# A two-pass channel scaling kernel: 26 rows fewer kept between the passes and loaded again ahead of the second pass, and the arena moved to the front of its pool

## The chip, the cores and the metric

The kernel runs on one core of one Trainium2 chip. A core has a matrix engine (PE, or TensorE), a vector engine (DVE), a scalar engine (ACT), a general engine (POOL), a queue processor (SP) that here does nothing but issue DMA transfers, 16 DMA engines, an on-chip memory of 128 partitions (SBUF) and a small accumulator memory (PSUM). The metric is the device time of one execution, in microseconds (us); lower is better. The time before is 722.07 us, the median of three runs (721.76, 722.07 and 722.96).

## What is computed

The input `x` is one image of 384 by 384 points with 384 channels in bf16, 113.2 MB. The mean of every channel over all points is multiplied by one number `w1d`, put through a sigmoid, and every point is then scaled, channel by channel, by the result:

```python
g = jnp.einsum("bhwc->bc", x) / (H * W)
s = jax.nn.sigmoid(g * w1d[0])          # k = 1: the padding and the loop over i fall away
return x * s[:, None, None, :]
```

No output can be written before all of the input has been read and summed. The input doesn't fit into SBUF, so a part of it has to be read twice.

## The kernel before, in words

**Rows and chunks.** The 147,456 points are cut into 1152 "rows". A row is one point, 384 channels or 768 bytes, on each of the 128 partitions: 98,304 bytes in all. A chunk of n rows is one DMA; `view` gives each partition n points that lie behind each other in HBM, so that a DMA is 128 runs of n times 768 bytes, eight on each of the 16 DMA engines. The trace calls such a run a packet.

**The arena.** One tile, `arena`, of 275 rows per partition (line 181) holds nearly everything. `QS` (line 152) and `RAW` (line 160) lay it out: five areas for packed groups, then the pieces U (8 rows), V (8), A (39), Y (8) and T (8). The pool gives its tiles addresses in the order in which they are made, each rounded up to 32 bytes per partition. What the framework itself keeps ends at byte 16,512 of a partition. Before, `ones` (256 bytes), `w_bf`, `w_sc`, `worst` and `odd` (32 each) stand ahead of the arena, which so begins at byte 16,896, which is 66 times 256. A row is three times 256 bytes, so every row begins at a multiple of 256 bytes.

**Pass one** reads all 1152 rows. PE sums them into one PSUM bank: `sum_rows` issues a matmul with a matrix of ones for each row. Three things happen to a row after that:

- 785 rows (`N_STREAM`) are only streamed: they are overwritten, and read again in pass two.
- 296 rows are kept packed, four rows in the room of three, in groups: `fold` (line 272) hides the bits of a fourth row in the exponent bits of three others, with DVE and ACT.
- 71 rows (`N_RAW`, line 164) are kept as they are, "raw", in U, V, A, Y and T.

The streamed rows of the end of pass one go through three slots of 13 rows in A (`SLOTS`, line 368; `S1`, `S2`, `S3`), in the order that the list `BETWEEN` gives (line 380). After the last of them, `take_raw` (line 414) loads the 71 raw rows into the same three slots, then V, U, Y and T. Y, T, U and V are scratch or landing room of the folds until then.

**The turn.** When the last matmul is done, ACT computes the sigmoid (line 422) into `s_bf`. From then on DVE can scale rows in place (`scale`, line 429, one instruction for n rows) and SP can store them (`store`, line 439).

**Pass two** is laid out by a planner that runs when the kernel is built (lines 540 to 717). It steps a simulated clock by 0.05 us, with a cost for each row moved (`ROW`, 0.2267 us), each load (`PER_LOAD`, 0.112) and each store (`PER_STORE`, 0.061), and a model of DVE's times (`TS`, `TT`). It keeps `landed`, the pieces that are in SBUF and can be scaled, in order; `moves`, the transfers that are under way; `turns`, the steps that unpack a folded group; and `idle`, the arena rows that are free. When a run of free rows is long enough (line 700), it issues a load of the next streamed rows into it. The order in which the planner emits is the order of each engine's queue; the waits are put in by the class `Flow` from the rows that each step reads and writes. All loads and stores of rows are issued by SP, on one queue and strictly in that order: an issue that waits for its rows holds all behind it. Each DMA uses one of 24 semaphores in turn.

At the start of pass two `landed` holds the raw rows, in the order Y, T, U, V and A (lines 594 to 599), in eight pieces of 4, 4, 8, 8, 8, 13, 13 and 13 rows.

Of the kernel before, what the change touches and what calls it, by code (L numbers as in the profile page):

```python
# [127 lines left out]
def kernel(  # L128
# [12 lines left out]
    P = nc.NUM_PARTITIONS  # L141
    B, H, W, C = x.shape
# [5 lines left out]
    bf16, f32, u16, u32 = x.dtype, mybir.dt.float32, mybir.dt.uint16, mybir.dt.uint32  # L148
# [8 lines left out]
        areas.append((base, 3 * q))  # L157
        base += 3 * q
    RAW = {}
    for name, n in (("U", 8), ("V", 8), ("A", 39), ("Y", 8), ("T", 8)):  # L160
        RAW[name] = (base, n)
        base += n
    ROWS = base
    N_RAW = sum(n for _, n in RAW.values())
    U, V, A, Y, T = (RAW[n][0] for n in "UVAYT")

    BANKED = len(QS)
    PS = 3 * Q_BANKS
# [2 lines left out]
    pool = ctx.enter_context(tc.tile_pool(name="sb", bufs=1))  # L171
    psum = ctx.enter_context(tc.tile_pool(name="psum", bufs=1, space=bass.MemoryType.PSUM))

    pieces = [(g, lo, min(PIECE, q - lo)) for g, q in enumerate(QS) for lo in range(0, q, PIECE)]

    ones = pool.tile([P, P], bf16, name="ones")
    w_bf = pool.tile([1, 1], bf16, name="w_bf")
    w_sc = pool.tile([P, 1], f32, name="w_sc")
    worst = pool.tile([P, 1], f32, name="worst")
    odd = pool.tile([P, 1], bf16, name="odd")  # L180
    arena = pool.tile([P, ROWS, C], bf16, name="arena")
    s_bf = pool.tile([P, C], bf16, name="s_bf")
    zeros = pool.tile([P, P], bf16, name="zeros")
    seen = pool.tile([P, 2 * len(pieces)], f32, name="seen")
    odd_i = pool.tile([P, 1], mybir.dt.int32, name="odd_i")
    bank0 = psum.tile([P, nc.PSUM_BANK_SIZE_BYTES // 4], f32, name="bank0")
    acc, votes = bank0[:, 0:C], bank0[:, C : C + 1]
# [6 lines left out]
    def view(t, r0, n):  # L194
        return t[r0 * P : (r0 + n) * P, :].rearrange("(p r) c -> p r c", r=n)

    def rows(lo, n):
        return [("a", r) for r in range(lo, lo + n)]
# [3 lines left out]

    N_STREAM = RPP - N_RAW - sum(4 * q for q in QS)
    r = N_STREAM
    c_group = []
    for q in QS:
        c_group.append((r, 4 * q))
        r += 4 * q
    c_raw = (r, N_RAW)
    assert r + N_RAW == RPP  # L210

# [3 lines left out]
    def load(chunk, a, lo=0, hi=None):  # L215

        r0, n = chunk
        hi = n if hi is None else hi
        fl.add(
            "SP",  # L220
            lambda: nc.sync.dma_start(out=arena[:, a : a + hi - lo, :], in_=view(xf, r0, n)[:, lo:hi, :]),  # L221
            writes=rows(a, hi - lo), dma=True,
        )

    def sum_rows(a, n):
        def emit(i, first, last):
            return nc.tensor.matmul(acc, lhsT=ones[:], rhs=arena[:, i, :], start=first, stop=last)  # L227

        for i in range(a, a + n):
            first, last = summed[0] == 0, summed[0] == RPP - 1  # L230
            fl.add(
                "PE", lambda i=i, f=first, l=last: emit(i, f, l),
                reads=[("a", i), "ones"], writes=["bank0"],
            )
            summed[0] += 1
# [132 lines left out]
    SLOTS = [(A + i, 13) for i in range(0, 39, 13)]  # L368
# [3 lines left out]
    S1, S2, S3 = ([slot] for slot in SLOTS)  # L372
    B3, B4, AA = ([area] for area in (areas[3], areas[4], (A, 39)))

    def halves(area):
        a, n = area
        return [(a, n // 2), (a + n // 2, n - n // 2)]
# [4 lines left out]
        ([], B3), ([], B4),  # L382
        ([], B3), ([], AA),
        ([], halves(areas[4])), ([], S1 + S2 + S3),
        (S1, S2, S3 + S1), (S2, S3, S1 + S2 + S3),
    ]
    between = sum(n for b in BETWEEN[1:] for where in b for _, n in where)
    at = 0
    for g, q in enumerate(QS[:BANKED]):
        for lo in range(0, q, 2 * PIECE):  # L390
            n = min(2 * PIECE, q - lo)
# [19 lines left out]
            at += 1  # L411
    assert streamed[0] == N_STREAM

    def take_raw(a, n):
        load(c_raw, a, a - U, a - U + n)
        sum_rows(a, n)

    for a, n in SLOTS + [(V, 8), (U, 8), (Y, 8), (T, 5), (T + 5, 3)]:
        take_raw(a, n)
    assert summed[0] == RPP  # L420

    fl.add(
# [6 lines left out]
    def scale(a, n):  # L429
        v = arena[:, a : a + n, :]  # L430
        fl.add(
            "DVE",
            lambda: nc.vector.tensor_tensor(  # L433
                out=v, in0=v, in1=s_bf[:, None, :].to_broadcast([P, n, C]), op=Op.mult
            ),
            reads=rows(a, n) + ["s_bf"], writes=rows(a, n),
        )
# [46 lines left out]
    def TT(n):  # L484
        return 0.15 + 0.2 * n
# [54 lines left out]
    ROW, PER_LOAD, PER_STORE = 0.2267, 0.112, 0.061  # L540
    LAT, SEEN, DT = 2.0, 1.5, 0.05
    PENDING, MERGE = 24.0, 12.0
    BIG, CAP, PART, LOW, LAST = 32, 48, 16, 9.0, 4.0
    BANKS_AT = 2
    now = dve_at = 0.0
    moves, waiting, over, acts = deque(), deque(), deque(), deque()
    landed = deque()
    idle = [False] * ROWS
    todo = 0
# [18 lines left out]
    def send(chunk, a, lo, hi, then, known=None):  # L568

        waiting.append((dve_at, hi - lo, then, chunk, a, lo, [] if known is None else known))  # L570

    def backlog():
        return sum(e[1] for e in moves) + ROW * sum(e[1] for e in waiting)

    def split(n, m):
        k = -(-n // m)
        cuts = [n * i // k for i in range(k + 1)]
        return list(zip(cuts, cuts[1:]))
# [12 lines left out]
        return f  # L591


    landed.append((c_raw, Y, Y - U, 4, False))
    landed.append((c_raw, Y + 4, Y - U + 4, 4, True))
    landed.append((c_raw, T, T - U, 8, True))
    landed.append((c_raw, U, 0, 8, True))
    for e, n in ((0, 8), (8, 13), (21, 13), (34, 13)):
        landed.append((c_raw, V + e, 8 + e, n, True))

    HALVES = (T, U)
    half = [True, True]
# [46 lines left out]
    while True:  # L649

        if dve_at <= now:
            ahead = backlog()
            can = bool(turns)
            if not can and (ahead >= PENDING or not landed):
                can = start_pair()
                if can and not asked:
                    verdict()
                    asked = True
            if landed and (ahead < PENDING or not can):
                chunk, a, lo, n, end = landed.popleft()  # L660
                scale(a, n)
                dve_at = now + TT(n)
                since = (a, lo) if since is None else since
                if end or ahead < MERGE:
                    b, first = since
                    send(chunk, b, first, lo + n, stored(b, lo + n - first))
                    since = None
            elif can:
                f, t, then = turns.popleft()
                f()  # L670
                dve_at = now + t
                if then:
                    then()
        while waiting and waiting[0][0] <= now:
            _, n, then, chunk, a, lo, known = waiting.popleft()
            known.append(store(chunk, a, lo, lo + n))
            moves.append([now + LAT, n * ROW + PER_STORE, then])
        if out_rows == total and not checked and all(half):
            checked = True
            fl.add("POOL", again, reads=["odd_i", "s_bf"], writes=rows(Y, N_OVER), after=written)  # L680
        while over and over[0][0] <= now:
            over.popleft()[1]()

        got = runs()
        if bank_at is None and len(line) <= len(QS) * 2 - BANKS_AT and got and max(got)[0] >= PS:
            a = max(got)[1]
            for i in range(a, a + PS):
                idle[i] = False
            back = arena[:, a : a + PS, :].rearrange("p r c -> p (r c)")
            for i, bk in enumerate(banks):  # L690
                lo, hi = i * BANK, min((i + 1) * BANK, PS * C)
                copy_bank(i, bk[:, 0 : hi - lo], back[:, lo:hi], [("bank", i)], rows(a, PS))
            bank_at = (a, now + 5.0)
            got = runs()

        if got and todo < N_STREAM:
            n, a = max(got)
            n = min(n, CAP, N_STREAM - todo)
            ahead = backlog()
            if n >= BIG or n == N_STREAM - todo or (ahead < LOW and n >= 8) or ahead < LAST:  # L700
                chunk = (todo, n)
                todo += n
                load(chunk, a)
                for i in range(a, a + n):
                    idle[i] = False
                parts = [(chunk, a + e, e, f - e, f == n) for e, f in split(n, PART)]
                moves.append([now + LAT, n * ROW + PER_LOAD, lambda parts=parts: landed.extend(parts)])

        if moves and moves[0][0] <= now:
            moves[0][1] -= DT  # L710
            if moves[0][1] <= 0:
                over.append((now + SEEN, moves.popleft()[2]))
        else:
            stall += DT
        if not (moves or waiting or over or landed or line or turns) and todo == N_STREAM:
            break
        now += DT
# [34 lines left out]
```

## Time and profile before

| | |
|---|---|
| median of three runs | 722.07 us |
| the profiled execution: its own time, span | 722.96 us, 721.2 us |
| DMA bytes, mean rate over the span | 303.87 MB, 421 GB/s |
| read from HBM, written to it | 190.41 MB, 113.25 MB |
| loads of rows, stores of rows | 82, 56 |
| DVE busy, PE busy, ACT busy | 69%, 30%, 16% |
| last 16 matmuls of the sum start, first scaling starts | 267.8 us, 271.2 us |
| last DMA packets | about 718 us |

The page counts one profiled execution. Its part 2 cuts the span into 40 slices of 18 us; the row DMA gives the mean busy share of the 16 DMA engines in tenths. A finer table, by windows of one microsecond, gives the same share as a number for each (a little over 1 is possible, as a packet is counted where it starts), and GB/s. In the timeline, a line gives start, duration, engine, source line, operation and how many instructions were merged, and in brackets the idle time before and what ended it.

### The profile page before, as it was taken

Reading aid. Unit: us, or ns where it says so; the run is one execution under the profiler, and the core shown is the slowest. Engines: PE = TensorE matmul, PEld = TensorE weight load, DVE = VectorE, ACT = ScalarE, POOL = GpSimd, SP = SyncE. Lnnn points to the kernel's source line nnn. Section 1 sums busy time; section 2 is a strip of 40 time slices with the busy share of each in tenths; the row PEclk is TensorE's granted clock in tenths of the full one; section 3 lists DMA queues with packets and bytes.
Section 4 is the critical chain, followed back from the end, with each engine's and each line's share of the span. In section 5 each row is a group of like instructions: output and inputs, shape, how many; then the busy total and the mean of one; then the engine's idle time right before and its main releaser. Section 6 shows DMA issues by size and latency. Waiting matters only on the chain.

```text
span 721.2 us, 3243 instructions
## 1 busy us (share of the span) xinstructions
PE 213.6 (30%) x1202; PEld 118.9 (16%) x1202; DVE 496.2 (69%) x469; ACT 115.4 (16%) x92; POOL 0.2 (0%) x4
## 2 busy tenths in 40 slices
PE   4677879889877780000000000000000000000000
PEld 2344445545444340000000000000000000000000
DVE  4600006887996729998999998999979994355330
ACT  3600004665774520000100000000000000000000
POOL 0000000000000000000000000000000000000000
PEclk9899999999999995555555555555555555555555
DMA  9999999999999988999999999999999999999997
GB/s 386 426 429 430 444 414 428 432 431 430 427 428 426 418 342 320 408 424 430 432 430 439 424 436 432 427 446 428 428 433 431 441 431 435 422 439 428 438 436 323
DMA packets 19890, 303.87 MB, mean 421 GB/s; under 512 B 2210, under 2 KB 2210, under 8 KB 6434
## 3 DMA queue, kind: packets, MB, share of 16 engines
q1 hardware_dynamic: 19872, 303.67, 98.7%
q8 instruction: 9, 0.15, 0.1%
q14 instruction: 7, 0.06, 0.0%
q10 hardware_dynamic: 2, 0.00, 0.0%
HBM read 190.41 MB, written 113.25 MB: 421 GB/s over the span
## 4 chain that ended last, share of the span: by engine, by line
DMA 56%; DVE 27%; PE 6%; another core or an unknown queue 4%; ACT 2%; SPq 1%; issue 0%; DVEq 0%
DMA arena<-in_x_dram 41%; DVE arena L433 18%; DMA out_dram<-arena 15%; DVE arena L251 6%; PE bank L227 6%; DVE arena L257 4%; ACT arena L291 2%; SPq L221 1%; ACT s_bf L424 0%; PE bank L505 0%; DVE odd L500 0%; DVE odd_i L509 0%; DVE worst L495 0%; DVEq L112 0%
## 5 line engine op out<-in xcount | busy, mean ns | idle before, releaser
L433 DVE TENSOR_TENSOR arena<-arena,s_bf 128x1536 bf16<-128x1536 bf16 (+8 forms) x102 | 241.8, 2411 | 71.8 <-DMA arena<-in_x_dram 57.5
L251 DVE TENSOR_SCALAR arena<-arena 128x1536 uint16<-128x1536 uint16 (+2 forms) x247 | 145.9, 634 | 111.6 <-DMA arena<-in_x_dram 100.8
L227 PE MATMUL bank<-arena,ones 128*128 128x384 bf16 x1152 | 205.4, 340 | 55.0 <-DMA arena<-in_x_dram 54.9
L227 PEld LDWEIGHTS bank<-arena,ones 128*128 128x128 bf16 x1152 | 114.0, 101 | 146.1 <-DMA arena<-in_x_dram 60.7
L257 DVE TENSOR_TENSOR arena<-arena 128x1536 uint16<-128x1536 uint16 (+2 forms) x114 | 121.0, 1062 | 10.3 <-PE bank L227 8.1
L291 ACT ACTIVATE arena<-arena 128x3072 uint16<-128x3072 uint16 (+1 forms) x38 | 102.5, 2696 | 146.1 <-DVE arena L251 146.1
L361 ACT COPY arena<-bank 128x512 uint32<-128x512 uint32 (+1 forms) x7 | 4.0, 571 | 70.5 <-DMA out_dram<-arena 70.3
L242 PE MATMUL bank<-ones,zeros 128*128 128x384 bf16 x48 | 8.3, 326 | 0.0
L291 ACT ACTIVATION_READ_ACCUMULATOR arena<-arena 128x1 f32 x38 | 7.1, 187 | 0.0
L242 PEld LDWEIGHTS bank<-ones,zeros 128*128 128x128 bf16 x48 | 4.7, 98 | 3.1
L505 PE MATMUL bank<-odd,ones 128*128 128x1 bf16 x1 | 0.2, 187 | 15.8 <-DVE odd L500 15.8
L361 ACT COPY bank<-arena 128x512 uint32<-128x512 uint32 (+1 forms) x7 | 3.6, 567 | 0.0
L505 PEld LDWEIGHTS bank<-odd,ones 128*128 128x128 bf16 x1 | 0.1, 106 | 16.2 <-DVE odd L500 16.2
L424 ACT ACTIVATE s_bf<-bank,w_sc 128x384 bf16<-128x384 f32 x1 | 0.6, 581 | 12.9 <-PE bank L227 12.9
L720 ACT ACT_TABLE_LOAD x1 | 1.3, 1283 | 0.7 <-PEq L736 0.7
L321 DVE TENSOR_SCALAR w_sc<-bank 128x1 f32<-128x1 f32 x1 | 0.2, 157 | 1.1 <-PE bank L316 1.1
L311 DVE MEMSET ones<- 128x128 bf16 x1 | 0.2, 165 | 1.0 <-SPq L106 1.0
L316 PE MATMUL bank<-w_bf,ones 1*128 1x1 bf16 x1 | 0.2, 181 | 2.1 <-DMA w_bf<-in_w1d_dram 2.1
L316 PEld LDWEIGHTS bank<-w_bf,ones 1*128 1x128 bf16 x1 | 0.1, 99 | 2.1 <-DMA w_bf<-in_w1d_dram 2.1
L509 DVE CAST odd_i<-bank 128x1 int32<-128x1 f32 x1 | 0.2, 158 | 0.3 <-PE bank L505 0.3
L495 DVE TENSOR_REDUCE worst<-seen 128x1 f32<-128x38 f32 x1 | 0.2, 182 | 0.0
L500 DVE TENSOR_SCALAR odd<-worst 128x1 bf16<-128x1 f32 x1 | 0.2, 156 | 0.0
(5 smaller groups left out, 0.5 us busy)
## 6 DMA issues: line engine op xcount, KB each, us to landing
arena<-in_x_dram SPq DMA_DIRECT2D x17, 4608.0 KB, 34.5
out_dram<-arena SPq DMA_DIRECT2D x6, 4608.0 KB, 43.9
arena<-in_x_dram SPq DMA_DIRECT2D x21, 1248.0 KB, 11.6
arena<-in_x_dram SPq DMA_DIRECT2D x9, 2304.0 KB, 27.3
out_dram<-arena SPq DMA_DIRECT2D x8, 2304.0 KB, 28.1
arena<-in_x_dram SPq DMA_DIRECT2D x4, 4512.0 KB, 33.6
out_dram<-arena SPq DMA_DIRECT2D x3, 4512.0 KB, 26.7
out_dram<-arena SPq DMA_DIRECT2D x9, 1248.0 KB, 12.0
```

The costliest lines, as they stand in the source:

```text
L221: lambda: nc.sync.dma_start(out=arena[:, a : a + hi - lo, :], in_=view(xf, r0, n)[:, lo:hi, :]),
L227: return nc.tensor.matmul(acc, lhsT=ones[:], rhs=arena[:, i, :], start=first, stop=last)
L242: lambda: nc.tensor.matmul(acc, lhsT=zeros[:], rhs=ones[:, None, :].to_broadcast([P, C // P, P]), start=False, stop=False),
L251: lambda: nc.vector.tensor_scalar(out=dst, in0=src, scalar1=s0, scalar2=s1, op0=op0, op1=op1),
L257: "DVE", lambda: nc.vector.tensor_tensor(out=dst, in0=a, in1=b, op=op), reads=reads, writes=writes
L291: lambda: nc.scalar.activation(out=y, in_=y, func=ACTF.Copy, accum_out=seen[:, 2 * k + i : 2 * k + i + 1]),
L316: lambda: nc.tensor.matmul(votes, lhsT=ones[0:1, :], rhs=w_bf[0:1, 0:1], start=True, stop=True),
L361: "ACT", lambda: nc.scalar.copy(dst.bitcast(u32), src.bitcast(u32)), reads=reads, writes=writes
L424: lambda: nc.scalar.activation(out=s_bf[:], in_=acc, func=ACTF.Sigmoid, scale=w_sc[:, 0:1]),
L433: lambda: nc.vector.tensor_tensor(out=v, in0=v, in1=s_bf[:, None, :].to_broadcast([P, n, C]), op=Op.mult),
L505: lambda: nc.tensor.matmul(votes, lhsT=ones[:], rhs=odd[:], start=True, stop=True),
L720: nc.scalar.preload_act_table(ACTF.Sigmoid)
```

## The change

Three things are edited.

1. **Order in the pool.** The arena is made first, ahead of `ones` and the other small tiles. It then begins at byte 16,512 of a partition, which is 64.5 times 256: every row begins 128 bytes past a multiple of 256.
2. **26 rows fewer are kept raw.** `N_RAW` is 45 instead of 71, `N_STREAM` 811 instead of 785. The 26 rows that were raw in the first two slots of A (`S1` and `S2`) are streamed through these slots in the same two loads of 13 rows (`BETWEEN` gets `S1 + S2` at its end). The raw rows begin at `HELD`, the third slot. When all loads of pass one have been issued, SP issues one more, of the first 26 streamed rows (`N_AHEAD`), into the first two slots of A: `load((0, N_AHEAD), A)`. It waits until PE has summed these slots' rows.
3. **The planner.** A comes first among the pieces, so that V lies between U and Y. Pass two starts with V, then Y and T (in three pieces), U and the third slot (in two pieces); the 26 rows loaded ahead come as two pieces of 13 when the planner takes them to have landed. Streamed rows are loaded from row 26 on. A small load is issued for a run of at least 12 free rows (8 before) when under 9 us of transfers are planned ahead, and for at least 8 (any before) when under 4 us are.

```diff
-    for name, n in (("U", 8), ("V", 8), ("A", 39), ("Y", 8), ("T", 8)):
+    for name, n in (("A", 39), ("U", 8), ("V", 8), ("Y", 8), ("T", 8)):
...
-    N_RAW = sum(n for _, n in RAW.values())
-    U, V, A, Y, T = (RAW[n][0] for n in "UVAYT")
+
+    N_AHEAD = 26
+    N_RAW = sum(n for _, n in RAW.values()) - N_AHEAD
+    A, U, V, Y, T = (RAW[n][0] for n in "AUVYT")
...
-
+    arena = pool.tile([P, ROWS, C], bf16, name="arena")
     ones = pool.tile([P, P], bf16, name="ones")
+    s_bf = pool.tile([P, C], bf16, name="s_bf")
     w_bf = pool.tile([1, 1], bf16, name="w_bf")
+    zeros = pool.tile([P, P], bf16, name="zeros")
     w_sc = pool.tile([P, 1], f32, name="w_sc")
+    seen = pool.tile([P, 2 * len(pieces)], f32, name="seen")
     worst = pool.tile([P, 1], f32, name="worst")
     odd = pool.tile([P, 1], bf16, name="odd")
-    arena = pool.tile([P, ROWS, C], bf16, name="arena")
-    s_bf = pool.tile([P, C], bf16, name="s_bf")
-    zeros = pool.tile([P, P], bf16, name="zeros")
-    seen = pool.tile([P, 2 * len(pieces)], f32, name="seen")
...
-        (S1, S2, S3 + S1), (S2, S3, S1 + S2 + S3),
+        (S1, S2, S3 + S1), (S2, S3, S1 + S2 + S3 + S1 + S2),
...
+    HELD = A + N_AHEAD
+
     def take_raw(a, n):
-        load(c_raw, a, a - U, a - U + n)
+        load(c_raw, a, a - HELD, a - HELD + n)
         sum_rows(a, n)
 
-    for a, n in SLOTS + [(V, 8), (U, 8), (Y, 8), (T, 5), (T + 5, 3)]:
+    for a, n in [(HELD, U - HELD), (V, 8), (U, 8), (Y, 8), (T, 5), (T + 5, 3)]:
         take_raw(a, n)
+
+    load((0, N_AHEAD), A)
...
+    AHEAD = N_AHEAD * ROW + PER_LOAD - 3.3
+    FIRST = 6
...
-    landed.append((c_raw, Y, Y - U, 4, False))
-    landed.append((c_raw, Y + 4, Y - U + 4, 4, True))
-    landed.append((c_raw, T, T - U, 8, True))
-    landed.append((c_raw, U, 0, 8, True))
-    for e, n in ((0, 8), (8, 13), (21, 13), (34, 13)):
-        landed.append((c_raw, V + e, 8 + e, n, True))
+    def parts(chunk, a):
+        n = chunk[1]
+        return [(chunk, a + e, e, f - e, f == n) for e, f in split(n, PART)]
+
+    for a, n, m in ((V, 8, 4), (Y, 16, FIRST), (U, 8, 8), (HELD, U - HELD, 8)):
+        for e, f in split(n, m):
+            landed.append((c_raw, a + e, a - HELD + e, f - e, f == n))
+    moves.append([0.0, AHEAD, lambda: landed.extend(parts((0, N_AHEAD), A))])
+    todo = N_AHEAD
...
-            if n >= BIG or n == N_STREAM - todo or (ahead < LOW and n >= 8) or ahead < LAST:
+            if n >= BIG or n == N_STREAM - todo or (ahead < LOW and n >= 12) or (ahead < LAST and n >= 8):
...
-                parts = [(chunk, a + e, e, f - e, f == n) for e, f in split(n, PART)]
-                moves.append([now + LAT, n * ROW + PER_LOAD, lambda parts=parts: landed.extend(parts)])
+                moves.append([now + LAT, n * ROW + PER_LOAD, lambda p=parts(chunk, a): landed.extend(p)])
```

## The prediction

> **What bounds the kernel now.** I read the page first, parts 2 and 3: which resource is never idle.
>
> ```profile
> DMA  9999999999999988999999999999999999999997
> GB/s 386 426 429 430 444 414 428 432 431 430 427 428 426 418 342 320 408 424 430 432 430 439 424 436 432 427 446 428 428 433 431 441 431 435 422 439 428 438 436 323
> ...
> q1 hardware_dynamic: 19872, 303.67, 98.7%
> ```
>
> The DMA engines are busy from end to end, on one queue, in both passes. DVE has 225 us without work and PE two thirds of the span. So the time is the sum of the transfers plus the stretches in which the DMA engines run dry. There is one such stretch, slices 15 and 16: 342 and 320 GB/s where 430 is usual. Next the windows of one microsecond over it (columns: window, length, busy time of PE, PEld, DVE, ACT and POOL, PE clock, DMA share, GB/s).
>
> ```profile
> 266.00:267.00 1.00, 1.00 (x7) 0.61 (x8) 0.00 (x0) 0.00 (x0) 0.00 (x0) 1.00 1.00 403
> 267.00:268.00 1.00, 0.63 (x5) 0.18 (x3) 0.00 (x0) 0.00 (x0) 0.00 (x0) 1.00 0.44 176
> 268.00:269.00 1.00, 1.00 (x8) 0.60 (x7) 0.00 (x0) 0.00 (x0) 0.00 (x0) 1.00 0.15 58
> 269.00:270.00 1.00, 1.00 (x8) 0.60 (x7) 0.00 (x0) 0.00 (x0) 0.00 (x0) 1.00 0.01 5
> ...
> 272.00:273.00 1.00, 0.00 (x0) 0.00 (x0) 1.00 (x3) 0.00 (x0) 0.00 (x0) 1.00 0.00 0
> 273.00:274.00 1.00, 0.00 (x0) 0.00 (x0) 1.00 (x2) 0.00 (x0) 0.00 (x0) 0.70 1.02 415
> ...
> 275.00:276.00 1.00, 0.00 (x0) 0.00 (x0) 1.00 (x1) 0.00 (x0) 0.00 (x0) 0.50 0.47 197
> ...
> 281.00:282.00 1.00, 0.00 (x0) 0.00 (x0) 1.00 (x1) 0.00 (x0) 0.00 (x0) 0.50 0.66 276
> ...
> 287.00:288.00 1.00, 0.00 (x0) 0.00 (x0) 1.00 (x3) 0.00 (x0) 0.00 (x0) 0.50 0.95 200
> 288.00:289.00 1.00, 0.00 (x0) 0.00 (x0) 1.00 (x2) 0.00 (x0) 0.00 (x0) 0.50 0.91 225
> 289.00:290.00 1.00, 0.00 (x0) 0.00 (x0) 0.97 (x3) 0.00 (x0) 0.00 (x0) 0.50 0.96 289
> ```
>
> The loads end in 267 to 269, and nothing moves until 273: 0.56 + 0.85 + 0.99 + 3.00 = 5.4 us idle. Two dips follow, 0.53 at 275 and 0.47 (with the next window) at 281, where each store waits for DVE. At 287 to 291 the engines are busy, but slow: 200, 225, 289, 393 GB/s, 1.4 us lost to packets that took up to three times their usual time. The timeline shows what the gap waits for.
>
> ```profile
> 267.76 2.77 PE L227 MATMUL bank<-arena,ones 128*128 128x384 bf16 x16 [0.37 <-DMA arena<-in_x_dram]
> 270.57 0.58 ACT L424 ACTIVATE s_bf<-bank,w_sc 128x384 bf16<-128x384 f32 x1 [12.90 <-PE bank L227]
> 271.18 14.84 DVE L433 TENSOR_TENSOR arena<-arena,s_bf 128x1536 bf16<-128x1536 bf16 x8 [13.60 <-ACT s_bf L424]
> 272.17 11.54 SPq L443 DMA_DIRECT2D out_dram<-arena  x7
> ```
>
> Last sums, sigmoid, first scaling, first store, and 0.85 us until its packets flow. Last, the price of a transfer: matmuls of 48-row loads start as these land, back to back.
>
> ```profile
> 60.66 9.65 PE L227 MATMUL bank<-arena,ones 128*128 128x384 bf16 x48 [2.89 <-DMA arena<-in_x_dram]
> 71.69 7.97 PE L227 MATMUL bank<-arena,ones 128*128 128x384 bf16 x48 [1.38 <-DMA arena<-in_x_dram]
> 82.55 9.49 PE L227 MATMUL bank<-arena,ones 128*128 128x384 bf16 x48 [2.89 <-DMA arena<-in_x_dram]
> 93.42 7.97 PE L227 MATMUL bank<-arena,ones 128*128 128x384 bf16 x48 [1.38 <-DMA arena<-in_x_dram]
> ```
>
> They are 10.92 us apart in the mean. The packets in the trace say the same: 36,864 bytes take 1364 ns (median), eight behind each other 10.91 us, and 9,984 bytes take 375 ns. So a byte takes 0.0368 ns on its engine, a packet 8 ns besides, a row 0.226 us.
>
> **The change, part by part.** Every DMA that is added counts in full unless it lies in the gap.
>
> *Pass one* issues the same loads in the same order and sizes; the two last streamed loads take the place of two raw ones. Cost nothing, apart from the addresses (below).
>
> *The load ahead* is one more DMA of 26 rows: 26 x 0.226 us = 5.9 us. SP issues it behind the raw loads (the last at 258.5). It waits for the sums of slots one and two. From 256.3 PE has 71 of the sum's rows left, and these slots are the first 26; the weight loads in the timeline give 2 + 9 + 15 of them by 262.0, so the issue falls at about 262.5, five microseconds before the queue runs dry at 267.9. It then fills the gap of 5.4 us and overshoots by 0.5. Nothing is queued behind it on SP but the stores, which wait for DVE until 272.2. The sums themselves read other rows, so the scale is ready at 271.2 as before.
>
> *What it replaces.* The 26 rows, read in pass one anyway, are now read twice, and pass two's later loads shrink by none: 785 rows are still to be loaded and 1152 to be stored after the gap. So its 5.9 us buy 5.4 us of gap, and what they can fill of the dips: the queue is 0.5 us late at the first store, which takes the dip at 275 (0.53). By DVE's pace (14.84 us for 71 rows in eight instructions, some 0.2 us a row and 0.08 each) the new pieces of 4, 4, 5, 5, 6, 8, 6 and 7 rows end at 272.1 to 280.9, each store is then issued before the one ahead of it has left the queue, and the first 13-row piece is late by 0.5 at most, which an 8-row load into V, freed some 276, covers. The sum of the refill: idle 5.4 + 1.0 less 5.9, a gain of 0.5 us. Ends: a gain of 1.9 if the slow packets at 287 vanish as well; a loss of 0.5 if the dips stay. I take the gain of 0.5, since the pieces' times leave no dip, and nothing shows why the slow packets would go.
>
> *Thresholds of the planner.* Fewer small loads, two or three more small stores: by 8 x 8 ns, five DMAs either way are 0.3 us. I take nothing.
>
> *The address.* Rows begin 128 bytes past a multiple of 256 instead of on it. No row of this trace stands so: the arena's rows and HBM's are all multiples of 256. For DVE, ACT and PE I take nothing: their instructions on rows at odd and even multiples of 256 have one duration (3351 ns in the mean, 3359 at most, for 16 rows). For the DMA it meets every packet, and every packet is on the path: 82 + 1 loads and some 58 stores, 141 DMAs of eight packets on each engine, 1128 packets in series. Lower end: nothing. Upper end: each packet costs as much as another packet's start, 8 ns: 9.0 us. Between them: each moves the 128 bytes by which it is off once more, 128 x 0.0368 = 4.7 ns, in all 5.3 us. The planner's own costs lean to the upper half: they charge a 48-row load 10.99 us and a store 10.94, where the trace shows 10.91, that is 0.08 and 0.03 us each, 8.4 us over 83 and 58, as if written for dearer packets. I take 5.3, the row that needs no assumption but that of 128 bytes.
>
> The Trainium skill ("DMA: Bandwidth & Descriptors", section "How a descriptor splits into AXI transactions") has a rule against this change: a read that doesn't start on a multiple of 256 bytes starts at the multiple below, and the unused bytes cost beats of 32 bytes. By it a store's packet of n rows would take 24n + 4 beats instead of 24n. It speaks of reads alone; on the stores only, that would be an estimated 2.2 us and a time of 723.8. No row here shows a packet off 256, so the trace neither agrees nor disagrees.
>
> **Sum.** The profiled execution took 722.96 us, a span of 721.2 and 1.8 around it: 722.96 - 0.5 + 5.3 = 727.8. It is 0.9 above the median of the three runs (its loads at 250 to 256 are slow by about 1 us), which I don't carry over: 722.07 + 4.8 = 726.9.
>
> **The rivals.**
>
> *The address costs nothing.* For it: the packets' times are those of bytes alone, with 8 ns each. Against it: the planner's dearer costs. Then the refill stands alone: 721.6 us, 720.2 if the slow packets go. This is the one on the other side; it decides when a packet pays under 2 ns.
>
> *Only one direction pays.* A store reads SBUF, a load writes it, and the trace can't say whether both pay. Stores alone: 464 packets x 4.7 ns = 2.2 us, 723.8. Loads alone: 664, 3.1 us, 724.7.
>
> *Each packet pays a whole start,* 8 ns: 721.6 + 9.0 = 730.6. For it the planner's costs; against it that a packet's start is shared by all its bytes, not by the 128.
>
> *The load ahead comes late,* because PE's sums lag. PE's granted clock was 0.5 from 256.3 to 259.5, a matmul each 0.32 us; were it to stay there, the 26 would be done at 264.6. An issue is in time until some 0.9 us before 267.9 (the first store's 0.85 us from issue to packets); after that each microsecond costs one, up to 5.9: with the address, 727 to 733. Against it: even the slow case has 2 us to spare.
>
> **How the numbers follow.** Both directions pay about 128 bytes: 0.42, 726.9 (its own range 724.5 to 729.5). A whole start: 0.15. One direction alone: 0.20, half of it within the bound. Nothing: 0.18, of which 0.06 with slow packets gone, under 720.6. Late load: 0.05. A measurement here tells 0.2% (1.4 us) from no change. Faster 0.06, same 0.20, slower 0.74. The range leaves out the lowest and the highest tenth: 721.2 to 731.0.
>
> **What would show it.** Step by step: DMA share near 1 in 267 to 273, with 26 rows landing at about 274; first store still issued near 272; HBM reads of 192.97 MB; no dip to 0.5 before 285. For the address: 48-row loads landing 10.95 us apart instead of 10.91, 9,984-byte packets at 380 ns instead of 375, end of pass one later by 56 x 0.038 = 2.1 us. If packets keep 375 ns, the address step is wrong and the time is near 721.6; if DMA share stays under 0.9 near 270, the refill is.

## The result and the profile after

The changed kernel takes 730.41 us, the median of four runs (729.33 to 733.83), where the kernel before takes 722.32: 1.2% slower, a ratio of 1.012 with a 95% interval from 1.008 to 1.016. Six later runs gave 730.22 and 1.0121 (1.0097 to 1.0144). The forecast was 726.9, with 721.2 to 731.0 as its range: the measured time lies inside the range, 3.5 us above the forecast. The profiled execution took 729.33 us, 6.4 more than the one before; its span is 727.5.

The page first, the rows of DMA and rate, and the totals.

```profile
DMA  9999999999999999999999999999999999999996
GB/s 379 429 434 433 428 419 428 431 428 428 425 424 421 412 416 375 425 410 427 427 430 437 412 435 420 439 414 439 427 436 427 425 445 424 430 445 428 427 436 274
...
q1 hardware_dynamic: 21168, 306.23, 99.3%
...
HBM read 192.97 MB, written 113.25 MB: 421 GB/s over the span
```

The dent at the turn is gone from the DMA row, and 2.56 MB more are read. What is new is the last slice: 274 GB/s, where before had 323. The windows of one microsecond over the turn:

```profile
269.00:270.00 1.00, 1.00 (x8) 0.58 (x6) 0.00 (x0) 0.00 (x0) 0.00 (x0) 1.00 1.03 435
270.00:271.00 1.00, 1.00 (x8) 0.59 (x7) 0.00 (x0) 0.00 (x0) 0.00 (x0) 1.00 1.17 502
271.00:272.00 1.00, 0.49 (x4) 0.10 (x1) 0.00 (x0) 0.47 (x1) 0.00 (x0) 1.00 0.89 379
272.00:273.00 1.00, 0.00 (x0) 0.00 (x0) 0.86 (x1) 0.11 (x1) 0.00 (x0) 1.00 1.02 439
...
280.00:281.00 1.00, 0.00 (x0) 0.00 (x0) 1.00 (x2) 0.00 (x0) 0.00 (x0) 0.50 1.53 280
281.00:282.00 1.00, 0.00 (x0) 0.00 (x0) 1.00 (x2) 0.00 (x0) 0.00 (x0) 0.50 0.95 100
282.00:283.00 1.00, 0.00 (x0) 0.00 (x0) 1.00 (x1) 0.00 (x0) 0.00 (x0) 0.50 0.39 129
```

The load ahead fills the gap as forecast: the share stays near 1 through 273 (274 to 275 has 0.70). But the slow stretch that stood at 287 has only moved, to 280 to 283: 280, 100 and 129 GB/s. There the first load of pass two (8 rows, into V) stands between stores, and its packets take up to 2.2 us where 234 ns is usual. The chain of the turn is the old one, about 1 us later, in the timeline:

```profile
268.72 2.77 PE L228 MATMUL bank<-arena,ones 128*128 128x384 bf16 x16 [0.40 <-DMA arena<-in_x_dram]
271.53 0.58 ACT L429 ACTIVATE s_bf<-bank,w_sc 128x384 bf16<-128x384 f32 x1 [12.22 <-PE bank L228]
272.14 3.97 DVE L438 TENSOR_TENSOR arena<-arena,s_bf 128x1536 bf16<-128x1536 bf16 x4 [12.93 <-ACT s_bf L429]
273.13 2.27 SPq L448 DMA_DIRECT2D out_dram<-arena  x3
```

A finer scale than the windows is the landing of each DMA: its 16 semaphore increments, as many as there are DMA engines; I take each to be one engine's. I give their mean, and how far the last stands behind the mean ("spread"). By it, the profiled executions of before and after compare so:

| | before | after | difference |
|---|---|---|---|
| last raw load, mean | 267.95 | 269.45 | 1.5 |
| first store, mean | 274.39 | 276.34 | 2.0 |
| last store, mean | 717.70 | 721.90 | 4.2 |
| last store, slowest engine | 719.26 | 725.97 | 6.7 |

(The tail behind the last store is 0.3 us shorter, which makes it 6.4 in the span.) So of the 6.7 us, 1.5 arise in pass one, which issues the same loads as before, 0.5 at the turn and 2.2 in pass two, and 2.5 are that the slowest engine ends 4.1 us behind the mean instead of 1.6. The windows show this as a tail. Before, the last four microseconds; then after, from 716 in steps of two:

```profile
716.00:718.00 2.00, 0.00 (x0) 0.00 (x0) 0.00 (x0) 0.00 (x0) 0.00 (x0) 0.50 0.52 221
718.00:720.00 2.00, 0.00 (x0) 0.00 (x0) 0.00 (x0) 0.00 (x0) 0.00 (x0) 0.50 0.03 14
```

```profile
716.00:718.00 2.00, 0.00 (x0) 0.00 (x0) 0.00 (x0) 0.00 (x0) 0.00 (x0) 0.50 1.03 442
718.00:720.00 2.00, 0.00 (x0) 0.00 (x0) 0.00 (x0) 0.00 (x0) 0.00 (x0) 0.50 0.76 327
720.00:722.00 2.00, 0.00 (x0) 0.00 (x0) 0.00 (x0) 0.00 (x0) 0.00 (x0) 0.50 0.43 184
722.00:724.00 2.00, 0.00 (x0) 0.00 (x0) 0.00 (x0) 0.00 (x0) 0.00 (x0) 0.50 0.28 120
724.00:726.00 2.00, 0.00 (x0) 0.00 (x0) 0.00 (x0) 0.00 (x0) 0.00 (x0) 0.50 0.09 37
```

### The profile page after: what moved, and what is told of

It is laid out like the page before. It is cut to its first block, busy times and chain, and to the rows that moved or that the text cites. A ratio compares the mean times of both kernels' runs of the same rounds, so it can differ in the third digit from the quotient of the medians.

```text
span 727.5 us, 3255 instructions
## 1 busy us (share of the span) xinstructions
PE 215.8 (30%) x1202; PEld 119.6 (16%) x1202; DVE 496.7 (68%) x472; ACT 115.4 (16%) x92; POOL 0.2 (0%) x4
## 4 chain that ended last, share of the span: by engine, by line
DMA 67%; DVE 19%; PE 6%; ACT 2%; SPq 1%; issue 0%; DVEq 0%
DMA arena<-in_x_dram 43%; DMA out_dram<-arena 24%; DVE arena L438 13%; PE bank L228 6%; DVE arena L252 4%; DVE arena L258 2%; ACT arena L292 2%; SPq L222 1%; ACT s_bf L429 0%; SPq L448 0%; PE bank L510 0%; DVE odd L505 0%; DVE worst L500 0%; DVEq L112 0%; DVE odd_i L514 0%
## 5 line engine op out<-in xcount | busy, mean ns | idle before, releaser
L228 PE MATMUL bank<-arena,ones 128*128 128x384 bf16 x1152 | 207.7, 342 | 53.7 <-DMA arena<-in_x_dram 53.7
```

## The experiments

### Address and load ahead, each alone

Three kernels. The first is the changed one with the small tiles ahead of the arena again:

```diff
-    arena = pool.tile([P, ROWS, C], bf16, name="arena")
     ones = pool.tile([P, P], bf16, name="ones")
-    s_bf = pool.tile([P, C], bf16, name="s_bf")
     w_bf = pool.tile([1, 1], bf16, name="w_bf")
-    zeros = pool.tile([P, P], bf16, name="zeros")
     w_sc = pool.tile([P, 1], f32, name="w_sc")
-    seen = pool.tile([P, 2 * len(pieces)], f32, name="seen")
     worst = pool.tile([P, 1], f32, name="worst")
     odd = pool.tile([P, 1], bf16, name="odd")
+    arena = pool.tile([P, ROWS, C], bf16, name="arena")
+    s_bf = pool.tile([P, C], bf16, name="s_bf")
+    zeros = pool.tile([P, P], bf16, name="zeros")
+    seen = pool.tile([P, 2 * len(pieces)], f32, name="seen")
```

> The changed kernel with the pool's order of before: the arena begins at byte 16,896 again, a multiple of 256; the load ahead and its plan stay. Theory A (the rows' address makes all of the loss: a small price on each load, seen as 0.037 us in pass one, and the packets of pass two that take 100 to 500 ns too long): 721.6 us, between 720.6 and 722.8; load landings in pass one 2.98 us apart for 13 rows instead of 3.01; no spread of more than 2 us between the DMA engines at the end. Theory B (the small price is the address's, but the slow packets and the spread of 4 us between the engines at the end come from the load ahead: without an idle stretch at the turn the engines no longer draw level, and the new plan mixes loads and stores in another way): 727 us, between 725.5 and 728.5, with the spread at the end still near 4 us.

Measured: 725.11 us (723.16 to 726.82) against 722.91, ratio 1.0036 (1.0023 to 1.0050). That is what neither theory said. The address accounts for most of the loss, but not for all; without it the change is still slower. The spread at the end is 1.5 us, so the spread isn't the load ahead's, as theory B had it.

The second is the kernel before with the pool's order of the changed one, and nothing else, so the same lines the other way round (the other small tiles move with it):

```diff
+    arena = pool.tile([P, ROWS, C], bf16, name="arena")
     ones = pool.tile([P, P], bf16, name="ones")
...
-    arena = pool.tile([P, ROWS, C], bf16, name="arena")
```

> The kernel before, with only the arena made first, so that every row begins 128 bytes past a multiple of 256; 71 raw rows, no load ahead. Theory A: 730 us, between 728 and 732, loads 13 rows 3.01 us apart in pass one, slow packets in pass two. Theory B: 722.3 and 82 loads x 0.037 = 725.4, between 724.5 and 726.2, without slow packets in pass two, since the idle stretch of 5.4 us lets the engines draw level.

Measured: 728.40 us (727.93 to 730.25), ratio 1.0082 (1.0069 to 1.0096): 5.5 us for the address alone, at the lower edge of theory A's range and well above B's. By the landings its profiled execution falls behind the kernel before by 1.3 us in pass one, 0.3 at the turn, 2.7 in pass two and 1.2 by the spread at the end. The third has two tiles ahead of the arena, so that rows stand 192 bytes past a multiple of 256; its edit against the second:

```diff
+    w_bf = pool.tile([1, 1], bf16, name="w_bf")
+    w_sc = pool.tile([P, 1], f32, name="w_sc")
     arena = pool.tile([P, ROWS, C], bf16, name="arena")
     ones = pool.tile([P, P], bf16, name="ones")
...
-    w_bf = pool.tile([1, 1], bf16, name="w_bf")
...
-    w_sc = pool.tile([P, 1], f32, name="w_sc")
```

> As the run before, but with two small tiles of 32 bytes ahead of the arena: rows begin 192 bytes past a multiple of 256. If only being off 256 counts: the same as at 128, within 1 us (about 730 by theory A, 725.4 by theory B). If the bytes up to the next multiple are what is paid (64 now, 128 there): half of the loss, 726 by A, 724 by B. If the bytes behind the last multiple are paid (192): one and a half times the loss, 734 by A, 727 by B.

Measured: 729.95 us (728.24 to 730.77), ratio 1.0093 (1.0078 to 1.0108). The intervals of the two overlap; neither half nor one and a half of the loss fits. Between 128 and 192 bytes past a multiple of 256 these runs can't tell a difference; other distances weren't run.

A control came last: the kernel before with `zeros` made ahead of the arena, which moves every address by 256 bytes.

```diff
     ones = pool.tile([P, P], bf16, name="ones")
+    zeros = pool.tile([P, P], bf16, name="zeros")
     w_bf = pool.tile([1, 1], bf16, name="w_bf")
...
     s_bf = pool.tile([P, C], bf16, name="s_bf")
-    zeros = pool.tile([P, P], bf16, name="zeros")
```

> The kernel before, with the 256 bytes of the tile of zeros made ahead of the arena: every address of the arena moves by 256, so that rows stay on multiples of 256 (a control for the runs with rows 128 and 192 past it, which were 0.8 and 0.9% slower). If being off a multiple of 256 is what costs: as before, 722.7, within 0.8; 13-row loads of pass one 2.98 us apart. If any other arrangement of the arena costs: 726 to 730, loads 3.01 us apart.

Measured: 722.79 us against 722.79, ratio 1.0001 (0.9993 to 1.0010). So it isn't that the arena was moved, but that its rows no longer begin on multiples of 256. Pass one shows the price at its plainest. Matmuls of three loads of 13 rows start as these land; the control's, then the ones of the kernel with rows 128 past 256:

```profile
245.60 2.29 PE L227 MATMUL bank<-arena,ones 128*128 128x384 bf16 x13 [1.21 <-DMA arena<-in_x_dram]
248.62 2.29 PE L227 MATMUL bank<-arena,ones 128*128 128x384 bf16 x13 [0.73 <-DMA arena<-in_x_dram]
251.60 2.29 PE L227 MATMUL bank<-arena,ones 128*128 128x384 bf16 x13 [0.69 <-DMA arena<-in_x_dram]
```

```profile
247.19 2.29 PE L227 MATMUL bank<-arena,ones 128*128 128x384 bf16 x13 [1.30 <-DMA arena<-in_x_dram]
250.20 2.29 PE L227 MATMUL bank<-arena,ones 128*128 128x384 bf16 x13 [0.72 <-DMA arena<-in_x_dram]
253.21 2.29 PE L227 MATMUL bank<-arena,ones 128*128 128x384 bf16 x13 [0.72 <-DMA arena<-in_x_dram]
```

A matmul starts when the slowest engine's part is in, so the mean landings say it better. Medians between back-to-back loads of pass one, in all traces: 13 rows 2.98 us where rows begin on 256 (eight traces) and 3.01 where they don't (five); 24 rows 5.46 to 5.47 and 5.50; 48 rows 10.89 and 10.92. It is 0.030 to 0.036 us a load, much the same for all three sizes, at 128 and at 192. Stores of 48 rows behind another store (two or three in a trace) take 10.89 us in the median on 256, and 10.88 off it: a store pays nothing.

### What is left without the address

The first experiment left 2.2 us. Its kernel differs from before by the load ahead and by the planner's thresholds. Three kernels take these apart: the first experiment's with the old thresholds; the kernel before with the new thresholds (the same line the other way round); and the first experiment's with 13 rows ahead instead of 26.

```diff
-            if n >= BIG or n == N_STREAM - todo or (ahead < LOW and n >= 12) or (ahead < LAST and n >= 8):
+            if n >= BIG or n == N_STREAM - todo or (ahead < LOW and n >= 8) or ahead < LAST:
```

> The load ahead with the arena on multiples of 256 (the first experiment), and the planner's thresholds for small loads as before the change (at least 8 free rows under 9 us of planned transfers, any under 4). It asks why that experiment was 2.2 us slower than before and not 0.5 faster. Theory C (the second reading of 26 rows, 5.9 us, is more than the gap gives back): as the first experiment, 725, between 724 and 726. Theory D (the plan: the other thresholds cut pass two in ways that cost time): the loss goes, 722.5, between 721.5 and 723.5. Theory F (without an idle stretch at the turn the DMA engines don't draw level, and slow packets add up in some runs): 725, with runs that spread over 2 us or more.

Measured: 722.69 us (721.91 to 723.23) against 722.60, ratio 1.0004 (0.9995 to 1.0013). Theory D. The load ahead with 26 rows read twice costs and brings nothing that these runs can tell.

> The kernel before with nothing changed but the thresholds for small loads (at least 12 free rows under 9 us, at least 8 under 4). Theory C: as before, 722.9, within 0.7. Theory D: 2 us slower, 724.9, between 724 and 726. Theory F: as before, 722.9, all runs within 1 us.

Measured: 729.55 us (727.67 to 731.06), ratio 1.0094 (1.0078 to 1.0110). Theory D's sign, three times its size.

```diff
-    N_AHEAD = 26
+    N_AHEAD = 13
...
-        (S1, S2, S3 + S1), (S2, S3, S1 + S2 + S3 + S1 + S2),
+        (S1, S2, S3 + S1), (S2, S3, S1 + S2 + S3 + S1),
...
-    for a, n in [(HELD, U - HELD), (V, 8), (U, 8), (Y, 8), (T, 5), (T + 5, 3)]:
+    for a, n in [(HELD, 13), (HELD + 13, 13), (V, 8), (U, 8), (Y, 8), (T, 5), (T + 5, 3)]:
```

> The first experiment with 13 rows loaded ahead instead of 26 (58 raw rows; the load ahead takes 2.97 us and leaves some 2.4 us of the gap idle). Theory C: the gap is left partly idle, each row read twice is paid by gap that it fills: 723.5 to 724.5. Theory D: the plan's thresholds are still there: 724.5 to 726. Theory F: the idle stretch is back, so the engines draw level: 722.9, within 0.8, and runs within 1 us of each other.

Measured: 721.84 us (721.09 to 722.41), ratio 0.9986 (0.9977 to 0.9995). No theory had it faster. The new thresholds, still in it, cost nothing here (the run with the old ones, below, takes the same time). So it isn't the thresholds as such: each of the three plans is another plan, and some of them run the queue short. A second trace of the first experiment's kernel shows where:

> The first experiment's kernel once more, for a second trace: its five runs lay between 723.2 and 726.8, and the one with a trace was the fastest. Expected 723 to 727. If the run is above 724.5, the trace shows where: by theory C at the turn (267 to 300), by theory D in the small loads of 300 to 370, by theory F in loads of pass two whose packets take 100 ns or more too long, with a spread between engines at the end of over 2 us.

Measured: 724.71 us. Two windows of four microseconds of that trace, and the same two of the kernel with the old thresholds:

```profile
308.00:312.00 4.00, 0.00 (x0) 0.00 (x0) 4.00 (x3) 0.00 (x0) 0.00 (x0) 0.50 1.01 389
312.00:316.00 4.00, 0.00 (x0) 0.00 (x0) 2.95 (x2) 0.00 (x0) 0.00 (x0) 0.50 0.98 299
```

```profile
308.00:312.00 4.00, 0.00 (x0) 0.00 (x0) 4.00 (x3) 0.00 (x0) 0.00 (x0) 0.50 1.02 434
312.00:316.00 4.00, 0.00 (x0) 0.00 (x0) 4.00 (x4) 0.00 (x0) 0.00 (x0) 0.50 1.02 431
```

The waits of SP's queue from 300 to 320 give the reason, new thresholds first, then old:

```profile
SPq L222 <- DMA out_dram<-arena: 9.7, 2, 7.4
SPq L448 <- DVE arena L438: 3.5, 2, 3.1
```

```profile
SPq L448 <- DVE arena L438: 8.6, 4, 3.2
SPq L222 <- DMA out_dram<-arena: 6.3, 3, 3.0
```

With the new thresholds an issue of a 12-row load stands for 7.4 us at the head of SP's queue, waiting for the store out of its rows to land, at 309.1. Two stores behind it are issued only then, at 309.5 and 310.4; DVE had the rows of the first ready at 307.7, those of the second at 310.35. By then one store of 13 rows is nearly all that the DMA engines still have, and many of the load's packets take far longer than 347 ns: 1.45 us too long in all. (Here and below, this is the sum over the packets that take at least 100 ns more than others of their size, shared over 16 engines.) With the old thresholds a small load of 8 rows goes at 297.5 and the 12 rows go at 306.6, no such wait exceeds 3.0 us, and the packets of the 12 rows are 0.05 us too long. The wait alone isn't the price: with 13 rows ahead and the new thresholds the same load waits 6.3 us, and its packets are 0.05 us too long as well. In the kernel before with the new thresholds it is worse. First a window of the kernel before, then this one's windows from 298 and its waits from 295 to 330:

```profile
302.00:306.00 4.00, 0.00 (x0) 0.00 (x0) 3.96 (x5) 0.00 (x0) 0.00 (x0) 0.50 0.99 402
```

```profile
298.00:302.00 4.00, 0.00 (x0) 0.00 (x0) 3.97 (x5) 0.00 (x0) 0.00 (x0) 0.50 0.94 388
302.00:306.00 4.00, 0.00 (x0) 0.00 (x0) 4.00 (x2) 0.00 (x0) 0.00 (x0) 0.50 0.74 224
306.00:310.00 4.00, 0.00 (x0) 0.00 (x0) 4.00 (x4) 0.00 (x0) 0.00 (x0) 0.50 1.02 344
```

```profile
SPq L221 <- DMA out_dram<-arena: 21.9, 4, 8.5
SPq L443 <- DVE arena L433: 8.9, 6, 3.2
```

By 296 the kernel before has issued loads of 47 rows in pass two, this one of 29: the higher thresholds put loads off. Its next loads wait 21.9 us in four issues, one of them 8.5, and the engines run dry. Three of these loads (issued at 302.7, 313.1 and 324.9) have packets that are 1.4 to 1.7 us too long each. The transfers that land between 300 and 350 take 6.7 us more than their packets' usual times add up to, against 0.1 before. DVE has no idle time in these windows (3.97 to 4.00 of 4), so no store could have come much sooner: behind the first two of the three loads the next store's rows were ready only after the load's issue, by 1.2 and 0.6 us. What is missing here is loads, and not stores that were held back.

### Do the parts add up?

> The changed kernel as it is (arena first, 26 rows loaded ahead), with only the thresholds for small loads as before. If address, load ahead and thresholds add up (5.5 us, nothing and 2.4 us by the runs so far): 728.2 us against 722.6 for the kernel before, between 727 and 729.5. If the thresholds cost only where the queue is filled from rows on multiples of 256 (no adding up): as the changed kernel, 730.4, between 729.5 and 732.

Measured: 729.61 us (727.96 to 730.69), ratio 1.0090 (1.0076 to 1.0104). It lies 0.1 us over the range of the first case and as little inside that of the second, so it decides nothing by itself.

> The changed kernel unchanged, for a narrower interval than its four runs gave (1.012, from 1.008 to 1.016), beside the run with the old thresholds (729.6, 1.009). If the thresholds' 2.4 us are there with rows off 256 as well: 731 to 733. If they are lost in the address's own loss: 729 to 730.5.

Measured: 730.22 us (728.69 to 734.70), ratio 1.0121 (1.0097 to 1.0144). By the expectation the thresholds' loss is lost in the address's: 0.6 us is left by the medians. But by the ratios it is 0.3% (2.2 us), and the two intervals overlap and leave room for none or for up to 0.7%, so its size stays open. The traces show that it isn't all gone: the load of 12 rows that waits 7.4 us in the second trace of the first experiment waits 7.5 in both traces of the changed kernel, and its packets are 0.8 and 1.4 us too long, against 0.15 with the old thresholds.

> 13 rows loaded ahead, the arena on multiples of 256, old thresholds. If the old thresholds are better in themselves: 721.0 or below, under the 721.84 of the same kernel with the new ones. If it is each plan's chance where the queue runs short (the new ones cost 7 us with 71 raw rows, 2.4 with 26 rows ahead and nothing with 13): anything between 721.3 and 725, and an issue of a load that comes late shows where.

Measured: 721.74 us (721.06 to 722.13), ratio 0.9987 (0.9978 to 0.9996). As with the new thresholds: for this plan they make no difference. These two kernels with 13 rows ahead, the arena on multiples of 256, are the only ones faster than before, by 0.13 to 0.14%. What makes 13 better than 26 was not taken apart.

In numbers of the medians, then: the address costs 5.5 us with 71 raw rows and 6.9 with the load ahead (729.6 against 722.7), the load ahead nothing that can be told, the thresholds 2.4 with rows on 256 (725.1 against 722.7) and an unsettled amount with rows off.

## Why the prediction came out as it did

*Pass one issues the same loads, dearer by the address only:* right. It ends 1.5 us later, where 2.1 were forecast.

*The load ahead lies in the gap, the scale is not delayed by it, its bytes are not won back:* right. The issue fell at 262.35, as worked out (262.5); the load landed at 275.4, where about 274 was forecast. With the address and the thresholds taken out the whole part measures a loss of 0.1 us (ratio 1.0004, from 0.9995), where a gain of 0.5 was taken, just outside this interval. The dips were mostly filled, but the slow packets, of which "nothing shows why" they would go, did not go: 1.4 us were lost to them before, 1.8 at 280 to 283 now.

*Thresholds of the planner, "I take nothing":* wrong. The step counted DMAs (141 forecast, 147 issued) and priced each; it didn't ask when the plan lets each load go. The higher thresholds put loads off, a load then waits on SP for a store to land, and when it goes the engines have little left and its packets can be slow. This costs 2.4 us on aligned rows and 7 with another plan, far over the 0.3 that were bounded, and nothing with 13 rows ahead; in the changed kernel it is 0.6 by the medians and 2.2 by the ratios. That late loads and slow packets come together is shown; why such packets are slow is not.

*The address, 5.3 us:* its total was near (5.5 to 6.9) by luck, as its make-up was not as worked out. "Every packet is on the path", 4.7 ns each, for loads and stores: loads of pass one pay about 0.034 us for eight packets in a row, 4.3 ns each, which is 1.9 us for 56 loads; the landings give 1.1 to 1.5. Stores pay nothing. And this small price is hardly there in most of pass two: after 340 us at most 7% of the loads' packets take 2 ns or more over their usual time, in pass one 51% or more. The rest is something that no step had: in pass two some loads have a stretch in which about ten to twenty packets take 100 to 1400 ns too long. Here it is in the changed kernel, in the last packets of a load of 39 rows:

```profile
396.00:400.00 4.00, 0.00 (x0) 0.00 (x0) 4.00 (x2) 0.00 (x0) 0.00 (x0) 0.50 1.02 442
400.00:404.00 4.00, 0.00 (x0) 0.00 (x0) 4.00 (x5) 0.00 (x0) 0.00 (x0) 0.50 0.96 355
```

After 340 us, packets that are 100 ns or more too long add up to 1.4 to 2.4 us (shared over 16 engines) in all five traces with rows off 256, and to 0.1 to 0.5 in all eight with rows on it. Loads have nearly all of it: off 256 their part is 1.4 to 2.2 us, the stores' at most 0.3. With the address alone (the second experiment) it is 2.4 us against 0.1 before, which is most of the 2.7 lost in pass two. It doesn't fall on all engines alike: the spread at the last store is 2.8 to 5.6 us off 256 and 1.4 to 2.3 on it. That being off 256 brings it is shown by these runs; what in the chip stalls the packets is not. With 71 raw rows it struck the same three loads at 128 and at 192 bytes, those that land near 370, 451 and 545 us, which speaks against mere chance.

*The rule of the Trainium skill* ("DMA: Bandwidth & Descriptors", section "How a descriptor splits into AXI transactions") named the right boundary, 256 bytes. What it states of reads would make stores dearer, since they read SBUF; the traces have it the other way round, stores unchanged at 10.88 us for 48 rows and loads of pass one dearer by about 0.034 us. The measurement decides. The estimate from the rule, 723.8, was 6.6 us short.

*The rivals.* "The address costs nothing" and "stores alone pay" fell. "Each packet pays a whole start" gave 730.6, the measured time, by a mechanism that the packets refute: 8 ns more would be 383, but of the 1920 packets of 9,984 bytes in pass one of the changed kernel 539 still take 375 ns (1844 before), the others mostly 376 to 387, and their median is 379. "The load ahead comes late" did not happen.

*The signs named in advance.* 48-row loads came 10.92 us apart instead of 10.89 (0.04 more were forecast); the median packet of 9,984 bytes is 379 ns in the loads of pass one, where 380 was forecast, and 375 over the whole trace, in which the stores are counted too; the forecast that no window before 285 would dip to half failed at 282.

## What to carry to other kernels

Where a kernel is bound by its transfers, look at the address at which its buffers begin: here 128 bytes more or less in front of the arena were 0.8%, and the way to see it is the landing time of one load against another of the same size, and the longest packets, not the busy share, which was full in both. Data that is given up to fill an idle stretch of the DMA engines has to be read again on the same engines; here 26 rows brought nothing, and 13 rows 0.13%. A change of a planner's thresholds is a change of when each load goes: before pricing it by the count of transfers, look for the issue that will wait for another transfer to land, and for what the engines still have by then.

## What was not expected of the hardware

- The direction: back-to-back loads of pass one into SBUF rows that begin 128 or 192 bytes past a multiple of 256 take 0.030 to 0.036 us longer per DMA of 128 packets, at 13, 24 and 48 rows; 48-row stores out of them take the same time. The long stalls of pass two, too, fall on loads.
- The small price is not there from the first packet. In the changed kernel's trace, packets of 36,864 bytes take their 1364 ns to the nanosecond from 13 to 25 us, and begin to exceed it, by 3 to 4 ns in the mean, after 30 to 40 us. Why isn't known.
- The first loads of pass two, which come to engines that have had only stores for some time, have slow packets: at 288 to 291 in the kernel before up to 820 ns instead of 234, in the changed kernel up to 2.2 us. The plans traced here all have such a stretch in the first 30 us of pass two. Why isn't known.
- Runs of the kernel before lie within 1 to 2 us of each other; those with rows off 256 spread over 2 to 6 us. Being off 256 isn't the only thing that does it: the two kernels on 256 that the new thresholds slowed spread over 3.4 and 3.7 us.
